# Products of the first layer in 26 multiplications: new order of the pairs, sums made when needed, additions that read PSUM

## Chip, cores and metric

The kernel runs on one core of one Trainium2 chip. The metric is device time in microseconds (us), the median of several executions. PE is the matrix engine (TensorE; PEld are its weight loads), DVE is VectorE, ACT is ScalarE, POOL is GpSimd, SP is SyncE, which here only issues DMAs.

## The reference

```python
# q, k, v: (8 batches, 12 heads, 448 rows, 64); all float32
q_n, k_n = rmsnorm(q, g_q), rmsnorm(k, g_k)      # over the 64
scores = q_n @ k_n.T / 8
attn = softmax(scores)
x = (attn @ v)           # -> (8 * 448 tokens, 12 * 64 = 768)
h = x @ w_in             # w_in: 768 x 2048
g = h * sigmoid(h)       # SiLU
out = g @ w_out          # w_out: 2048 x 768
```

## The kernel before, in words

Attention runs in 24 *couples* (a couple is two pairs of heads of one batch, four heads); six couples are two batches, a *group*. Function `visit(c)` emits the scores (line 852), their exponentials on ACT (857) and the weighted sums (889) of couple c; `between(c)` emits what lies between two couples: the flips of the next q and k (782, 786), the sums of the weights (903) and their totals (932), and two calls of `fill`. `fill` takes matmuls of the first layer (`x @ w_in`) from a generator, a quota of columns per call, and deals a list of other small steps evenly between them; what it emits, in this order, is the order of every engine's queue. So couples 6 to 11 carry the first layer of batches 0 and 1, couples 12 to 17 that of 2 and 3, couples 18 to 23 that of 4 and 5; batches 6 and 7 are done alone, when attention is over. Last comes `out = g @ w_out` (`quad`, `deep`), which the change doesn't touch.

The groups of couples 6 to 17 use seven products in place of eight (class `Seven`). From couple 18 on `products_in` (line 1359) runs a scheme of 26 products for a 4 x 2 by 2 x 4 block product. `room.chunk(i)`, i from 0 to 3, holds a quarter of w_in, and each chunk needs 26 left factors (quarters of the chunk and sums of them, 128 x 384), 26 right factors (quarters of x and sums of them, 128 x 672), and additions of the products:

- `LEFT_SUMS`, `form(i)` (line 1179): 18 sums per chunk on DVE (line 1217), after a `restore` on POOL (1201). They are spread by `dealt` over the fills of couples 13 to 20. Six slots in `room.sums` rotate; `keep` (1193) stores each factor on SP's queue into `lefts` in DRAM (1197), 26 stores of 192 KB per chunk, in the places that the order of pairs asks for. A slot that comes round again waits for its store to land.
- `Ring` (1262): loads the two left factors of a pair (384 KB, line 1288) from `lefts` on ACT's queue into the next free slot. It starts at the end of couple 17 with seven slots, and gets five more when attention is over.
- `RIGHT_SUMS`, `sum_right` (1251): 18 sums per group, `EARLY_SUMS` (four) on POOL at the end of couple 17 or 23, `LATE_SUMS` (eight on DVE, six on POOL, line 1255) around the start of the products.
- `products_in`: thirteen pairs per chunk. A pair has two products of three matmuls, which the trace shows as twelve of 224 columns, into one bank of PSUM. ACT copies the bank to SBUF (1390, 1395). `combine` (1313) makes, one pair later, the additions that `AFTER` lists, 38 per chunk; 18 of them are marked for POOL, the rest go to DVE (line 1339). In the group that runs alone (`direct`) some of them read PSUM. A finished pair of outputs goes through SiLU (1308) and is saved in `hidden` (1310).
- `bank` (1040): in couples 18 to 23 the products take two banks named mm in turn, at times one of the scores' buffers (sc); alone there are eight.

In the `LAGGED` couples (10, 12 to 16, 18 to 22) the division by the total of the weights comes one couple later: `sum_up` (907) makes the totals in a bank mm, two reciprocals of 128 x 224 (941) and a copy (947) follow on DVE, and four DMAs on SP's queue (950) swap rows between the two factors; `divide` (960) uses them in the next couple.

`rounder` and `early` bring W_out into the form the products need, in pieces of 128 x 384: a load on SP (188), two steps on ACT (`open`, 203 and 204), three on DVE (226 to 233) and one on POOL (237). `early`, the first eight pieces, runs by `rounds` in couples 21 to 23; the other 24 run beside the products alone, from `prepare_out` (1507).

Of the kernel before, what the change touches and what calls it, by code (L numbers as in the profile page):

```python
# [35 lines left out]
)  # L36
FACTORS_LEFT = (
    18, 23, 22, 20, 3, 24, 11, 10, 2, 4, 25, 1, 16, 8, 14, 13, 17, 5, 9, 15, 21, 12, 2, 19, 3, 6,
# [7 lines left out]
}  # L46
FACTORS_RIGHT = (
    11, 1, 4, 12, 4, 0, 16, 24, 0, 3, 6, 22, 21, 19, 13, 17, 15, 7, 9, 14, 8, 25, 18, 10, 23, 20,
)


AFTER = {
    4: ((16, 100, "-", 104, 0),),
    6: ((22, 103, "+", 106, 0), (1, 22, "-", 102, 1)),
    7: ((17, 107, "-", 22, 0),),
    8: ((17, 17, "+", 108, 0), (4, 104, "+", 108, 1), (0, 102, "+", 17, 1)),
    12: ((18, 112, "-", 104, 0),),
    13: ((3, 113, "-", 111, 1),),
    16: (
        (23, 116, "-", 113, 0), (18, 18, "-", 23, 0), (14, 23, "-", 105, 0),  # L60
        (12, 105, "+", 18, 1), (8, 17, "+", 18, 1),
    ),
    17: ((27, 114, "+", 117, 0), (20, 27, "-", 106, 0), (11, 109, "+", 117, 1), (9, 101, "+", 27, 1)),
    18: (
        (24, 118, "-", 115, 0), (19, 108, "+", 24, 0), (14, 14, "+", 24, 0),
        (13, 20, "-", 118, 1), (9, 9, "-", 118, 1),
    ),
# [7 lines left out]
}  # L75
# [567 lines left out]
def bounded(  # L643
# [20 lines left out]
    hidden = dram.tile([z.NF, P, z.B * S], F32, name="hidden")  # L664

# [5 lines left out]
    work = mem.tile([P, 16 * S + z.NK], F32, name="work")  # L671
    at = 0
# [10 lines left out]
    r = [piece(S) for _ in range(2)]  # L683
# [223 lines left out]
    def sum_up(c):  # L907
# [50 lines left out]
        yield [lambda: invert(0), lambda: (invert(1), spread())]  # L958
# [216 lines left out]
    PAIRS = len(FACTORS_LEFT) // 2  # L1175
    lefts = dram.tile([room.NC, PAIRS, P, 2 * K3], F32, name="lefts")
    formed = []

    def form(i, engines):
# [3 lines left out]
        s = room.sums((0, 1, 1, 3)[i])  # L1183
        tiles = w.rearrange("p (r k f m) -> p r k f m", r=HW, k=2, f=room.CHUNK)
        slots = [s[:, ds(n * K3, K3)] for n in range(6)]
        held, order = {}, []
# [6 lines left out]
        def keep(n):  # L1193
            for q, name in enumerate(FACTORS_LEFT):
                if name == n:
                    dst = lefts[i, q // 2, :, ds(q % 2 * K3, K3)]
                    nc.sync.dma_start(dst.rearrange("p (r m) -> p r m", r=HW), source(n))

        def restore():
            halves = w.rearrange("p (c m r k) -> p c m r k", c=z.NW, m=2, r=2)[:, 0:HW]  # L1200
            nc.gpsimd.tensor_tensor(
                out=halves[:, :, :, 1], in0=halves[:, :, :, 0], in1=halves[:, :, :, 1],
                op=ALU.subtract,
            )

        def one(k):
            name, x, op, y = LEFT_SUMS[k]
            a, b = source(x), source(y)
            later = {n for _, x, _, y in LEFT_SUMS[k:] for n in (x, y)} | set(order)
            busy = {n for n in later if n in held}  # L1210
            at = next(n for n, t in enumerate(slots) if not any(held[m] is t for m in busy))
            slot = slots.pop(at)
            slots.append(slot)
            for old in [o for o, t in held.items() if t is slot]:
                del held[old]
            held[name] = slot
            engines[k % len(engines)].tensor_tensor(  # L1217
                out=source(name), in0=a, in1=b, op=ALU.subtract if op == "-" else ALU.add
            )
            if k < 4:  # L1220
                for n in (2 * k, 2 * k + 1):
                    keep(n)
            if order:
                keep(order.pop())
            order.append(name)
            if k == len(LEFT_SUMS) - 1:
                keep(order.pop())
                formed.append(i)
# [22 lines left out]
    def sum_right(group, engine, *names):  # L1251

        def one(name):
            x, op, y = RIGHT_SUMS[name]
            engine.tensor_tensor(  # L1255
                out=right_of(group, name), in0=right_of(group, x), in1=right_of(group, y),
                op=ALU.subtract if op == "-" else ALU.add,
            )

        return [lambda name=name: one(name) for name in names]  # L1260

    class Ring:
# [15 lines left out]
        def more(self):  # L1278
            while self.n < (z.B // 2 - 2) * room.NC * PAIRS:
# [8 lines left out]
                nc.scalar.dma_start(slot, lefts[i, t])  # L1288
# [11 lines left out]
    pending, silent = [], []  # L1300
# [12 lines left out]
    def combine(now):  # L1313


        if not pending:
            return
        at, group, f0, names, last, places, fresh = pending.pop(0)
        for q in names:
            for k, (name, x, op, y, engine) in enumerate(AFTER.get(q, ())):  # L1320
                a, b = (
                    fresh[n] if n in fresh and (n not in at or n == 100 + q) else blocks[at[n]]
                    for n in (x, y)
                )
                engine = engine and x not in fresh and y not in fresh
                spent = [n for n in (x, y) if last[n] == (q, k)]
                if name < 16:
                    pair = name // 2
                    if pair not in places:
                        places[pair] = blocks.pair()  # L1330
                    at[name] = places[pair][name % 2]
                elif name not in at:
                    gone = [n for n in spent if n >= 16 and n in at]
                    if gone:
                        at[name] = at[gone[0]]
                        spent.remove(gone[0])
                    else:
                        at[name] = blocks.single()
                (nc.gpsimd if engine else nc.vector).tensor_tensor(  # L1339
                    out=blocks[at[name]], in0=a, in1=b, op=ALU.subtract if op == "-" else ALU.add  # L1340
                )
                for n in spent:
                    if n >= 16 and n != name and n in at:
                        blocks.release(at[n])
                if name < 16 and last[name] == (q, k) and last.get(name ^ 1, (99,)) <= (q, k):
                    pair = name // 2
                    silent.append((now + 1, f0 + pair // 2, group[pair % 2], places[pair]))

    def last_uses():
        last = {}  # L1350
        for q in range(len(FACTORS_LEFT)):
            for k, (name, x, _, y, _) in enumerate(AFTER.get(q, ())):
                for n in (name, x, y):
                    last[n] = (q, k)
        return last
# [3 lines left out]
    def products_in(group, beside=lambda: None, direct=False):  # L1359


        last = last_uses()
        kept = {
            n for q in AFTER for _, x, _, y, _ in AFTER[q] for n in (x, y)
            if n >= 100 and (not direct or q // 2 != (n - 100) // 2 or n < max(x, y) == 100 + q)
        }
        rows = list(carried)
        carried.clear()
        for i in range(room.NC):
            at, places = {}, {}  # L1370
            for t in range(PAIRS):
                slot = stream.next()
                o = bank(S)
                for h in range(2):
                    beside()
                    b = right_of(group, FACTORS_RIGHT[2 * t + h])
# [28 lines left out]
    def settle():  # L1405
        while pending:
            combine(clock[0])
        activate_some(10**9, len(silent))
# [927 lines left out]
```

## Time and profile before

| | us |
|---|---|
| median of 3 executions | 1360.36 (1358.47 to 1362.15) |
| the profiled execution | 1361.65, span 1359.9 |
| couples 0 to 11 (to 306.9 of the span) | 306.9 |
| couple 12, couple 13 | 33.3, 34.6 |
| couples 14 to 17 | 154.5 |
| couples 18 to 23 | 244.1 |
| products alone | 129.5 |
| W_out | 457.0 |

Over the whole span PE is busy 95%, DVE 78%, ACT 39%, POOL 34%, and the mean granted PE clock is 0.977. An engine's busy share is a mean over stages, so the table of stretches in the next part is read instead: PE's busy time against a stretch's length says how long it waited, and the granted clock whether it ran at less than full speed in between. A row of a timeline ends, in brackets, with the idle time of the engine before the instruction and what ended that. In a group of instructions stand the tile written and the tiles read, partitions x elements, the count, busy time and the mean of one, then idle time before them with its causes.

### The profile page before, as it was taken

How to read it: one execution, taken by the hardware profiler on the slowest of the kernel's cores; microseconds unless marked ns; L12 is line 12 of the kernel's file. 1: busy time of each engine (PE TensorE's matmuls, PEld its weight loads, DVE VectorE, ACT ScalarE, POOL GpSimd, SP SyncE). 2: the span in 40 equal slices, each digit the busy share in tenths (PEclk: the TensorE clock that was granted, in tenths of full speed). 3: DMA queues.
4: the chain of work that ended last, by engine and by line, in shares of the span. 5: the costliest groups of instructions: out<-in, count | busy, mean ns of one | idle time of the engine just before them, and what ended most of it. 6: DMA issues, size and time to landing. Idle time of an engine off the chain costs nothing.

```text
span 1359.9 us, 21894 instructions
## 1 busy us (share of the span) xinstructions
PE 1290.1 (95%) x7788; PEld 956.8 (70%) x7788; DVE 1059.4 (78%) x1848; ACT 532.1 (39%) x968; POOL 455.7 (34%) x325
## 2 busy tenths in 40 slices
PE   9999999999999887969798799899999999999998
PEld 5444444544444443857575699876999999999998
DVE  6989788767686776777586888779878787878785
ACT  7875666645454453644665335420000000000000
POOL 7755364433443245545363665420000000000000
PEclk9999999999999898979998899999999999999999
DMA  9664456535476566697765577971413232322311
GB/s 242 172 179 124 124 137 152 123 85 114 122 192 174 157 181 203 179 253 211 220 166 172 185 261 257 314 265 43 129 60 111 74 98 74 103 83 94 117 56 38
DMA packets 308923, 205.63 MB, mean 151 GB/s; under 512 B 207588, under 2 KB 283492, under 8 KB 308804
## 3 DMA queue, kind: packets, MB, share of 16 engines
q1 hardware_dynamic: 293200, 162.13, 42.5%
q10 hardware_dynamic: 15284, 41.10, 9.3%
q8 instruction: 64, 1.05, 0.3%
q0 software_dynamic: 320, 0.90, 0.2%
q14 instruction: 55, 0.45, 0.1%
HBM read 136.25 MB, written 61.73 MB: 146 GB/s over the span
## 4 chain that ended last, share of the span: by engine, by line
PE 40%; DVE 11%; DMA 5%; POOL 3%; issue 2%; ACT 2%; SPq 0%; ACTq 0%; DVEq 0%; POOLq 0%
PE alone L1651 22%; PE mm L1651 7%; PE av L889 3%; PE sc L852 2%; PE alone L1689 2%; DMA W<-lefts 2%; DVE W L1339 2%; DVE mixed L1339 1%; POOL W L1339 1%; PE alone L1378 1%; DVE work L903 1%; DVE W L1255 1%; PE mm L1689 1%; PE mm L1378 1%; DMA hidden<-W 1%
## 5 line engine op out<-in xcount | busy, mean ns | idle before, releaser
L857 ACT ACTIVATE work<-sc,rms 128x448 f32<-128x448 f32 x318 | 181.7, 634 | 89.1 <-PE sc L852 79.1
L852 PE MATMUL sc<-work 64*64 64x448 f32 x1344 | 172.7, 554 | 2.0 <-ACT work L857 1.2
L889 PE MATMUL av<-work,rows 64*64 64x448 f32 x1272 | 161.0, 560 | 8.6 <-DVE av L865 8.6
L630 POOL DMA_DIRECT2D out_dram<-mixed x2 | 1.2, 592 | 445.4 <-DVE mixed L1012 445.4
L903 DVE TENSOR_TENSOR work<-work 128x896 f32<-128x896 f32 (+1 forms) x110 | 122.9, 1149 | 34.8 <-PE av L889 34.3
L603 POOL TENSOR_TENSOR rms<-rms,minus_half 128x14 f32<-128x14 f32 (+4 forms) x40 | 99.2, 2482 | 100.2 <-DVE rms L599 96.2
L889 PEld LDWEIGHTS av<-work,rows 64*64 64x64 f32 x1272 | 67.6, 137 | 74.5 <-issue 26.1
L1651 PE MATMUL alone<-W,x 128*128 128x192 f32 x544 | 111.0, 326 | 0.0
L852 PEld LDWEIGHTS sc<-work 64*64 64x64 f32 x1344 | 60.8, 135 | 66.7 <-ACT work L857 26.8
L1065 PE MATMUL mm<-x,W 128*128 128x448 f32 x234 | 95.3, 543 | 1.8 <-DVE mixed L1012 1.8
L1651 PEld LDWEIGHTS alone<-W,x 128*128 128x128 f32 x544 | 92.2, 190 | 0.0
L1065 PE MATMUL mm<-sums_x,W 128*128 128x448 f32 x204 | 84.5, 548 | 5.8 <-DVE mixed L1012 5.8
L822 POOL TENSOR_TENSOR rms<-rms,minus_half 128x28 f32<-128x28 f32 x15 | 72.9, 4857 | 40.2 <-DVE rms L819 40.2
L1065 PEld LDWEIGHTS mm<-x,W 128*128 128x128 f32 x234 | 43.6, 190 | 46.9 <-issue 40.0
L1065 PEld LDWEIGHTS mm<-sums_x,W 128*128 128x128 f32 x204 | 38.1, 191 | 46.6 <-issue 35.9
L1661 ACT COPY sums_x<-alone 128x192 f32<-128x192 f32 x33 | 10.5, 317 | 141.6 <-PE alone L1651 136.7
L237 POOL TENSOR_TENSOR W<-W 128x512 int32<-128x512 int32 (+1 forms) x30 | 39.6, 1319 | 65.3 <-DVE W L233 41.1
L1065 PE MATMUL sc<-x,W 128*128 128x448 f32 x150 | 60.7, 540 | 0.0
L1665 ACT COPY x<-alone 128x192 f32<-128x192 f32 x34 | 10.8, 318 | 122.6 <-PE alone L1651 113.8
L1217 DVE TENSOR_TENSOR W<-W 128x384 f32<-128x384 f32 x72 | 44.8, 646 | 17.2 <-DMA lefts<-W 13.2
L575 DVE TENSOR_REDUCE rms<-rows 128x8 f32<-128x512 f32 (+2 forms) x50 | 32.0, 639 | 32.9 <-ACT rows L574 32.5
L1651 PE MATMUL alone<-W,work 128*128 128x192 f32 x244 | 56.3, 326 | 0.0
(381 smaller groups left out, 3026.7 us busy)
## 6 DMA issues: line engine op xcount, KB each, us to landing
W<-lefts ACTq DMA_DIRECT2D x68, 384.0 KB, 4.2
lefts<-W SPq DMA_DIRECT2D x104, 192.0 KB, 2.7
x<-hidden SPq DMA_DIRECT2D x14, 1024.0 KB, 5.3
hidden<-mixed SPq DMA_DIRECT2D x31, 448.0 KB, 3.2
W<-in_moe_w_in_dram SPq DMA_DIRECT2D x22, 512.0 KB, 6.1
rows<-in_moe_w_out_dram SPq DMA_DIRECT2D x24, 384.0 KB, 4.7
work<-lefts ACTq DMA_DIRECT2D x24, 384.0 KB, 5.1
hidden<-mixed SPq DMA_DIRECT2D x33, 224.0 KB, 4.3
```

The costliest lines, as they stand in the source:

```text
L237: nc.gpsimd.tensor_tensor(out=wi, in0=wi, in1=low, op=ALU.add)
L603: nc.gpsimd.tensor_tensor(out=t, in0=t, in1=half, op=ALU.pow)
L822: nc.gpsimd.tensor_tensor(out=f, in0=f, in1=minus_half.to_broadcast([P, n]), op=ALU.pow)
L852: nc.tensor.matmul(two[ds(half * D, D), h, 0:S], keys[rows, ts(half, D)], qT[rows, pair, :], start=True, stop=True,)
L857: nc.scalar.activation(left_weights(c)[:, h] if j == LEFT else weights(c, j)[:, i, h], two[:, h, 0:S], AF.Exp, scale=norm.column(c, i, h, j),)
L889: nc.tensor.matmul(sums[i][ds(h * D, D), :], v, w, start=(j == 0 and step == 1), stop=(j == LEFT - 1 and step == 1),)
L903: nc.vector.tensor_tensor(out=total, in0=total, in1=more, op=ALU.add)
L1065: nc.tensor.matmul(t, self.left(name, s), self.right(name, s), start=s == ends[0], stop=s == ends[1])
L1217: engines[k % len(engines)].tensor_tensor(out=source(name), in0=a, in1=b, op=ALU.subtract if op == "-" else ALU.add)
L1339: (nc.gpsimd if engine else nc.vector).tensor_tensor(out=blocks[at[name]], in0=a, in1=b, op=ALU.subtract if op == "-" else ALU.add)
L1651: nc.tensor.matmul(t, x[:, i], y, start=i == ORDER[0], stop=i == ORDER[-1])
L1689: nc.tensor.matmul(o, a[:, 2 * i + m, t], right_one(name, i)[:, m], start=n == 0, stop=n == len(steps) - 1,)
```

## The change

The scheme of 26 products stays. What it does:

- `STEPS` gives a new order of the pairs, `AFTER` a new order of the additions. An operand -1 or -2 is the second or first half of the pair's bank, -3 the whole bank; a name in brackets is a pair made by one instruction of 448 columns; "=" is a copy on ACT, five per chunk in all. The other 33 additions per chunk (28 of 224 columns, five of 448) all run on DVE, at once behind their pair's matmuls, and 17 of them read PSUM.
- `NEEDS`: the fourteen late sums of x are made on DVE by `products_in`, ahead of the first eleven pairs of chunk 0. The four early ones go to DVE too.
- `form`: sums are made three to an area, stored by one DMA of 576 KB; six quarters of the chunk are stored singly, so 12 stores per chunk. Chunks 0 and 3 have two areas, chunks 1 and 2 six. `restore` runs on DVE. A pair's load picks its two factors out of `lefts`, in two runs per partition. Chunk 3's forms lie in couples 18 to 21.
- The first seven loads of the ring go on SP's queue, three of them at the end of couple 16.
- In couples 18 to 22 the totals use a buffer sc; ACT copies them, one row of each goes by DMA into a tile of 128 x 14, DVE inverts that, and two DMAs spread it through DRAM (`totals`) to all partitions.
- The eight early pieces of W_out run in couples 22 and 23, their first load at the end of couple 21.

```diff
+STEPS = (
+    ((3, 22), (4, 4)),
+    ((5, 11), (7, 16)),
+    ((18, 2), (11, 0)),
...
+    ((25, 3), (6, 23)),
 )
+AFTER = (
+    ((16, "=", -2, 0), (17, "=", -1, 0),),
+    ((18, "=", -2, 0), (19, "=", -1, 0),),
+    ((20, "-", -2, 16), (21, "=", -1, 0), (4, "+", 16, -1),),
+    (((22, 23), "+", (18, 19), -3), (24, "-", 22, 19), (25, "-", 23, 17),),
...
+    (((34, 35), "-", (30, 31), -3), (36, "+", 26, 34), (37, "+", 35, 33), (8, "+", 29, 36), (2, "+", 30, 37),),
...
+    ((10, "+", -2, 37), (14, "-", 43, -1), (6, "-", -1, 46),),
 )
+NEEDS = ((9, 13), (10, 15), (21, 20), (19,), (8,), (14,), (17,), (25,), (22,), (18,), (23,))
...
-        elif c in LAGGED:
+        elif c in LAGGED and c < 3 * GROUP:
             t = ps_mm.tile([P, BANK], F32, name="mm")[:, 0:S]
...
-        yield [lambda: invert(0), lambda: (invert(1), spread())]
+        def gather():
+            nc.scalar.copy(r[0], t)
+            rows = r[0].rearrange("(n p) s -> n p s", n=4)[:, 0]
+            nc.sync.dma_start(spot, rows.rearrange("n (p e) -> n p e", p=P // 4))
+
+        def invert_all():
+            d = totals[c % 2]
+            nc.vector.reciprocal(out=spot, in_=spot)
+            nc.sync.dma_start(d.rearrange("n (p e) -> (n p) e", p=P // 4), spot)
+            source = d.rearrange("(h one i) s -> h one (i s)", one=1, i=2)
+            nc.sync.dma_start(both_r, source.to_broadcast([2, D, 2 * S]))
+
+        yield [gather, invert_all] if c in LAGGED else [lambda: invert(0), lambda: (invert(1), spread())]
...
+        free = (
+            (room.sums(0),), (room.sums(0), room.sums(1), room.chunk(0)),
+            (room.sums(0), room.sums(1), room.chunk(1)), (room.sums(3),),
+        )[i]
+        areas = [a[:, ds(k * 3 * K3, 3 * K3)] for a in free for k in range(2)]
...
         def one(k):
             name, x, op, y = LEFT_SUMS[k]
+            area = areas[k // 3 % len(areas)]
+            held[name] = area[:, ds(k % 3 * K3, K3)]
+            (plus if op == "+" else minus)(source(x), source(y), source(name))
+            if k < SIX:
+                kept = lefts[i, :, ds(k * K3, K3)].rearrange("p (r m) -> p r m", r=HW)
+                nc.sync.dma_start(kept, source(k + 1))
+            if k % 3 == 2:
+                nc.sync.dma_start(lefts[i, :, ds((SIX + k - 2) * K3, 3 * K3)], area)
...
-                nc.scalar.dma_start(slot, lefts[i, t])
+                a, b = sorted(position[n] for n in STEPS[t][0])
+                source = lefts[i].rearrange("p (n k) -> p n k", k=K3)[:, a : b + 1 : b - a]
+                queue.dma_start(slot.rearrange("p (n k) -> p n k", k=K3), source)
...
+        row = AFTER[t]
+        joined = tuple(a[0] for a in row if a[1] == "=")
+        if len(joined) == 2:
+            nc.scalar.copy(block(joined), both)
+        for k, (name, op, x, y) in enumerate(row):
...
+            a, b = operand(x), operand(y)
+            (plus if op == "+" else minus)(a, b, block(name))
...
+            for t, (_, rights) in enumerate(STEPS):
+                if i == 0 and t < len(NEEDS):
+                    run_all(sum_right(group, nc.vector, *NEEDS[t]))
+                o = bank(S)
...
                 now = clock[0] = clock[0] + 1
...
+                combine(t, at, places, o, group, i * room.CHUNK, now)
                 stream.done(slot)
-                combine(now)
...
-        21: (2, 7), 22: (2, 6), 23: (2, 6), 26: (3, 5), 27: (3, 5), 28: (3, 5), 29: (3, 4),
+        21: (2, 7), 22: (2, 6), 23: (2, 6),
     }
-    rounds = {30: 3, 31: 3, 32: 3, 33: 3, 34: 3, 35: 1}
+    dealt.update((i, (3, n)) for i, n in zip(range(25, 32), (4, 3, 3, 3, 3, 3, 0)))
+    rounds = {32: 4, 33: 4, 34: 4, 35: 4}
...
+        if c == OLD + GROUP - 2:
+            stream.add(room.sums(2))
+            stream.more(nc.sync)
         if c in LAGGED:
             lagging.extend(next(sum_up(c)))
+            if c >= 3 * GROUP:
+                lagging.pop(0)()
+                lagging.insert(0, lambda: None)
```

Keys of `dealt` and `rounds` are half couples: i is 2 (c - 6), plus 1 for the second fill of couple c.

More of the change, by code (lines that the diff above doesn't have):

```diff
@@ L664, in bounded @@
     hidden = dram.tile([z.NF, P, z.B * S], F32, name="hidden")
+    totals = [dram.tile([4, S], F32, name=f"totals{i}") for i in range(2)]
     sets = [mem.tile([P, 2 * z.NW * S], F32, name=f"x{i}") for i in range(2)]
@@ L671, in bounded @@
     work = mem.tile([P, 16 * S + z.NK], F32, name="work")
+    spot = mem.tile([P, 4 * S // P], F32, name="spot")
     at = 0
@@ L681, in bounded @@
     e = [piece(4 * S).rearrange("p (i h s) -> p i h s", i=2, h=2) for _ in range(3)]
-    r = [piece(S) for _ in range(2)]
+    both_r = piece(2 * S)
+    r = [both_r[:, ts(i, S)] for i in range(2)]
     extra, at = sets[1], 0
@@ L1174, in bounded, with form @@
     T = S // 2
-    PAIRS = len(FACTORS_LEFT) // 2
-    lefts = dram.tile([room.NC, PAIRS, P, 2 * K3], F32, name="lefts")
+    PAIRS = len(STEPS)
+    SIX = 6
+    position = {n: n - 1 for n in range(1, SIX + 1)}
+    position.update((t[0], SIX + k) for k, t in enumerate(LEFT_SUMS))
+    lefts = dram.tile([room.NC, P, len(position) * K3], F32, name="lefts")
     formed = []
-    def form(i, engines):
+    def form(i):
         w = room.chunk(i)
-        s = room.sums((0, 1, 1, 3)[i])
+        free = (
[3 more added lines that the diff above has]
+        areas = [a[:, ds(k * 3 * K3, 3 * K3)] for a in free for k in range(2)]
         tiles = w.rearrange("p (r k f m) -> p r k f m", r=HW, k=2, f=room.CHUNK)
-        slots = [s[:, ds(n * K3, K3)] for n in range(6)]
-        held, order = {}, []
+        held = {}
         def source(n):
@@ L1191, in source @@
             return held[n].rearrange("p (r m) -> p r m", r=HW)
[L1193 to L1197, printed above, removed]
         def restore():
             halves = w.rearrange("p (c m r k) -> p c m r k", c=z.NW, m=2, r=2)[:, 0:HW]
[L1201 to L1204, printed above, removed]
+            minus(halves[:, :, :, 0], halves[:, :, :, 1], halves[:, :, :, 1])
         def one(k):
             name, x, op, y = LEFT_SUMS[k]
[L1208 to L1225, printed above, removed]
+            area = areas[k // 3 % len(areas)]
[6 more added lines that the diff above has]
+                nc.sync.dma_start(lefts[i, :, ds((SIX + k - 2) * K3, 3 * K3)], area)
             if k == len(LEFT_SUMS) - 1:
-                keep(order.pop())
                 formed.append(i)
@@ L1276, in add, with more @@
             return new
-        def more(self):
+        def more(self, queue=nc.scalar):
             while self.n < (z.B // 2 - 2) * room.NC * PAIRS:
@@ L1311, in activate_some @@
             blocks.release(*two)
[L1313 to L1355, printed above, removed]
-    clock = [0]
[L1359 to L1366, printed above, removed]
+    def named(*operands):
+        return {n for x in operands for n in (x if isinstance(x, tuple) else (x,)) if n >= 0}
@@ new lines, in bounded, with combine, block, operand @@
+    last_use = {}
+    for t, row in enumerate(AFTER):
+        for k, (_, op, x, y) in enumerate(row):
+            if op != "=":
+                last_use.update(dict.fromkeys(named(x, y), (t, k)))
+    def combine(t, at, places, o, group, f0, now):
+        both = o.rearrange("p (two s) -> p two s", two=2)
+        def block(name):
+            if isinstance(name, tuple):
+                at.update(zip(name, blocks.pair()))
+                return blocks.two(*(at[n] for n in name))
+            if name < 16:
+                pair = name // 2
+                if pair not in places:
+                    places[pair] = blocks.pair()
+                at[name] = places[pair][name % 2]
+            else:
+                at[name] = blocks.single()
+            return blocks[at[name]]
+        def operand(n):
+            if isinstance(n, tuple):
+                return blocks.two(*(at[m] for m in n))
+            return both if n == -3 else o[:, ts(n + 2, T)] if n < 0 else blocks[at[n]]
+        row = AFTER[t]
[3 more added lines that the diff above has]
+        for k, (name, op, x, y) in enumerate(row):
+            if op == "=":
+                if len(joined) == 1:
+                    nc.scalar.copy(block(name), operand(x))
+                continue
+            a, b = operand(x), operand(y)
+            (plus if op == "+" else minus)(a, b, block(name))
+            for n in named(x, y):
+                if n >= 16 and last_use[n] == (t, k):
+                    blocks.release(at.pop(n))
+            if not isinstance(name, tuple) and name < 16 and name ^ 1 in at:
+                pair = name // 2
+                silent.append((now + 1, f0 + pair // 2, group[pair % 2], places[pair]))
@@ L1367, in products_in @@
+    clock = [0]
+    def products_in(group, beside=lambda: None):
         rows = list(carried)
@@ L1405, in settle @@
     def settle():
-        while pending:
-            combine(clock[0])
         activate_some(10**9, len(silent))
@@ L2117, in bounded @@
     slots = prepare_out()
-    run(products_in(group, lambda: run_all(next(slots, ())), direct=True))
+    run(products_in(group, lambda: run_all(next(slots, ()))))
     for more in slots:
```

81 lines of the change are left out of this document (23 added, 58 removed), and 31 rows, old and new, of tables (AFTER, LEFT_SUMS, RIGHT_SUMS).

## Prediction

> **What bounds the kernel now.** I read busy time by stretches, cut at the first score product of each couple of head pairs (couples 14 to 23) and at the end of attention. Columns: window, length, busy time (instructions) of PE, PEld, DVE, ACT, POOL, granted clock, DMA share, GB/s.
>
> ```profile
> 374.80:408.00 33.20, 33.20 (x186) 16.64 (x182) 27.47 (x41) 17.13 (x28) 14.10 (x7) 1.00 0.70 189
> 408.00:449.00 41.00, 35.16 (x188) 16.39 (x185) 26.35 (x40) 18.94 (x29) 13.54 (x6) 0.94 0.66 176
> 449.00:487.50 38.50, 34.60 (x184) 16.99 (x182) 27.24 (x39) 16.60 (x26) 15.10 (x7) 0.97 0.59 174
> 487.50:529.30 41.80, 33.89 (x188) 16.76 (x185) 35.96 (x44) 15.78 (x26) 20.16 (x11) 0.96 0.61 168
> 529.30:564.20 34.90, 33.88 (x224) 24.23 (x224) 22.93 (x30) 20.05 (x33) 14.77 (x7) 0.95 0.81 233
> 564.20:610.70 46.50, 35.77 (x234) 27.35 (x230) 31.45 (x46) 22.77 (x41) 29.37 (x25) 0.86 0.77 205
> 610.70:648.20 37.50, 34.14 (x236) 26.78 (x232) 28.65 (x44) 16.35 (x29) 18.75 (x14) 0.94 0.79 222
> 648.20:689.90 41.70, 35.42 (x232) 27.41 (x234) 25.77 (x41) 26.05 (x47) 19.23 (x17) 0.92 0.77 218
> 689.90:727.80 37.90, 32.88 (x229) 25.48 (x229) 29.89 (x43) 23.19 (x42) 22.47 (x21) 0.95 0.67 183
> 727.80:773.40 45.60, 37.03 (x253) 25.97 (x249) 33.96 (x42) 18.14 (x33) 21.98 (x22) 0.87 0.44 137
> 773.40:902.90 129.50, 122.28 (x625) 119.93 (x626) 109.55 (x208) 54.64 (x118) 70.99 (x71) 0.98 0.80 273
> ```
>
> Couple 14 is the measure: PE is never idle in 33.2 us, and VectorE is idle 33.2 - 27.5 = 5.7 us of them. Couples 15 to 17 do the same work in 121.3, that is 21.7 over 3 x 33.2. Couples 18 to 22 need 32.9 of PE each (the least row) and couple 23 needs 37.0: 201.4 against 244.1, so 42.7 over. The products alone (773 to 903) are nearly full. What follows, 457 us of W_out, the change leaves alone. So 64 us lie in nine couples, and the long waits there name their reason (start, duration, instruction, idle time before it and what ended it):
>
> ```profile
> 445.50 1.11 PE L1065 MATMUL mm<-sums_x,W 128*128 128x448 f32 x1 [5.84 <-DVE mixed L1012]
> 528.77 0.42 PE L818 MATMUL sc<-rms,ident 64*64 64x28 f32 x4 [7.80 <-DVE rms L805]
> 609.04 0.98 PE L932 MATMUL mm<-work,ones 128*32 128x448 f32 x4 [6.91 <-ACT mixed L1390]
> 680.32 0.74 PE L1378 MATMUL mm<-sums_x,W 128*128 128x224 f32 x1 [5.48 <-ACT W L1390]
> 771.62 1.02 PE L889 MATMUL av<-work,rows 64*64 64x448 f32 x4 [8.57 <-DVE av L865]
> 604.89 1.15 DVE L1217 TENSOR_TENSOR W<-W 128x384 f32<-128x384 f32 x2 [5.58 <-DMA lefts<-W]
> 608.55 0.56 DVE L1217 TENSOR_TENSOR W<-W 128x384 f32<-128x384 f32 x1 [1.49 <-DMA lefts<-W]
> 678.35 0.54 ACT L203 ACTIVATE W<-W 128x384 int32<-128x384 uint32 x1 [7.96 <-DMA W<-in_moe_w_out_dram]
> L1217 DVE TENSOR_TENSOR W<-W 128x384 f32<-128x384 f32 x72 | 44.8, 646 | 17.2 <-DMA lefts<-W 13.2 <-POOL W L1201 3.4
> ```
>
> PE waits for VectorE, or for a ScalarE that waits for VectorE. VectorE in turn stands in its forming of weight sums (L1217), 13.2 us until a store of an earlier sum frees the slot and 3.4 for GpSimd's restore. The reader is to see the pairs: 604.89 on VectorE leads to 609.04 on PE.
>
> **The change part by part. Prices first:**
>
> ```profile
> 774.61 0.85 DVE L1255 TENSOR_TENSOR W<-x 128x672 f32<-128x672 f32 x1
> 774.84 2.09 POOL L1255 TENSOR_TENSOR sums_x<-x 128x672 f32<-128x672 f32 x1 [2.21 <-DVE x L963]
> 775.49 2.16 DVE L1255 TENSOR_TENSOR W<-x,W 128x672 f32<-128x672 f32 x1
> L1339 DVE TENSOR_TENSOR W<-W,alone 128x224 f32<-128x224 f32 x18 | 6.6, 380 | 2.3 <-POOL W L1339 2.1
> L1339 DVE TENSOR_TENSOR mixed<-W 128x224 f32<-128x224 f32 x3 | 1.1, 379 | 0.0
> L1012 DVE TENSOR_TENSOR mixed<-mm,mixed 128x448 f32<-128x448 f32 x57 | 34.7, 609 | 11.2 <-PE mm L1065 4.9 <-ACT mixed L1455 3.5 <-POOL mixed L1089 1.9
> 487.50:529.30 41.80, 10.22 (x12) 0.96 0.61 168
> 529.30:564.20 34.90, 3.00 (x5) 0.36 (x1) 0.95 0.81 233
> 529.30:773.40 244.10, 46.27 (x79) 56.71 (x70) 0.91 0.70 198
> 773.40:902.90 129.50, 41.53 (x110) 33.26 (x41) 0.98 0.80 273
> 529.30:773.40 244.10, 7.94 (x8) 16.86 (x10) 0.91 0.70 198
> 773.40:902.90 129.50, 11.89 (x8) 12.43 (x6) 0.98 0.80 273
> L941 DVE RECIPROCAL work<-mm 128x224 f32<-128x224 f32 x10 | 15.5, 1548 | 1.8 <-PE mm L932 1.8
> L947 DVE COPY work<-work 128x448 f32<-128x448 f32 x6 | 3.9, 651 | 0.2
> L1378 PEld LDWEIGHTS alone<-x,W 128*128 128x128 f32 x72 | 13.6, 190 | 0.0
> 527.17 6.25 ACTq L1288 DMA_DIRECT2D W<-lefts  x7
> hidden<-mixed SPq DMA_DIRECT2D x31, 448.0 KB, 3.2
> lefts<-W SPq DMA_DIRECT2D x104, 192.0 KB, 2.7
> W<-lefts ACTq DMA_DIRECT2D x68, 384.0 KB, 4.2
> ```
>
> The window rows are busy times of single lines: L1217 in couple 17; L1339 in couple 18, in 18 to 23 and alone (DVE, then POOL); L1255 in the last two of these.
>
> The first three rows show a collision: a VectorE addition of 672 columns takes 0.85 us by itself and 2.16 while GpSimd adds. A 224-column addition takes 0.38, from SBUF alone or with one operand in PSUM. Every addition that leaves GpSimd therefore costs VectorE 0.38 and frees its neighbours.
>
> *Forms in threes (couples 13 to 21).* Stores fall from 26 to 12 per chunk, and slots from six in rotation to eighteen for chunks 1 and 2. There no sum waits for a store. Where there are two areas (chunks 0 and 3), one comes round half a couple later, against 2.7 us of landing for a third of what it holds. Couple 15's 5.84 goes down to about 1, and with it most of the cold clock (0.94 of 41.0): -6.5. In couple 16 the restore moves to VectorE, which no longer waits for GpSimd: -3. In couple 17 twelve sums fall from 10.2 to 12 x 0.56 = 6.7, but four sums of x come over from GpSimd (4 x 0.86 = 3.4), so its 7.8 us wait mostly stays: -1.5. Together -11. The bounds are -5 (one wait alone) and -21.7 (all of it).
>
> *Additions from PSUM.* A chunk has thirteen pairs, each freeing its bank before by ScalarE's copy. Now a chunk has 28 narrow additions and 5 of 448 columns on VectorE, 28 x 0.38 + 5 x 0.61 = 13.7 us, and 5 copies on ScalarE instead of about 13. Four chunks are 54.8; VectorE had 46.3 in couples 18 to 23 and 41.5 alone, with GpSimd's 56.7 and 33.3 beside it.
>
> [...]
>
> *Lazy sums of x.* All fourteen go to VectorE, in the first eleven pairs of chunk 0, two pairs or more ahead of their use: 14 x 0.86 = 12.0 against 7.9 and 11.9 before. GpSimd loses 16.9 and 12.4.
>
> *Lagged totals (couples 18 to 22).* Ten reciprocals (15.5) and five copies (5 x 0.65 = 3.3) go, five reciprocals of 14 columns (1 together) and a ScalarE copy come. SP now waits twice, for the small reciprocal and for the landing of the totals. Queued behind are v loads, saves of hidden and stores of forms, all wanted a quarter of a couple later or more. I take nothing; without that cover it is the last rival.
>
> *Loads.* The first seven leave ScalarE's queue (6.25 us of issue at couple 18's start) for SP's. Each later load is two runs: between 0 and 2 x 2.7 - 4.2 = 1.2 us more to land, behind seven slots. I take 0; in the stretch alone, with five slots more, up to 6.
>
> *W_out pieces.* They leave couple 21. The second one's load is still issued only after the first is rounded, so of 680.32's 5.48 I keep 4 in couple 22.
>
> Sum for couples 18 to 23. VectorE had 172.7; + 54.8 - 46.3; - 15.5 - 3.3 + 1; sums + 12.0 + 3.4 (early ones in couple 23) - 7.9; comes to 170.9. With 5.7 idle per couple that is 205.1, level with PE's 201.4, so no slack for uneven loads. Couple 18 is uneven: 22.9 - 3.0 - 7.9 + 7.0 (8.7 pairs) + 12 sums x 0.86 + four form steps (2.6) = 31.9, with idle time 37.6 against 34.9 now. It gets slower; 19 to 21 gain. I add 4 (W_out), 4 (half of 771.62's, as GpSimd's part is gone) and 8 of the remaining 22 us of small waits and cold clock: 221, or -23. The bounds are 201 and 256 (second rival).
>
> Sum alone. PE needs 624 x 0.19 = 118.6. VectorE comes to 109.6 - 41.5 + 54.8 - 11.9 + 12.0 = 123.0, less what GpSimd's absence saves. The first chunk holds 13.7 + 12.0 + 14.0 (a quarter of the other 56.2) = 39.7 against 29.7 of PE; two pairs of lead are 4.6, relief 2, so +3. The bounds are -8 and +12.
>
> Total: -11 - 23 + 3 = -31. From the profiled execution, 1361.65 (span 1359.9 and 1.75 around it; 1.3 above the median of 1360.36), that is **1330**.
>
> **Rivals.**
>
> *All waits gone.* PE becomes the only bound, as the lower bounds of the three stretches have it: 1361.7 - 21.7 - 42.7 - 8 = 1289. For it: couple 14 shows that it can be. Against it: VectorE at 205.1.
>
> *VectorE in the turn of the banks.* Couples 18 to 23 have two banks for products. A bank now comes free after VectorE's additions, which stand in order behind flips, sums and rounding; ScalarE's copy stood behind little. If VectorE lags by more than one pair (12 x 0.19 = 2.3 us), every pair shows its additions: 52 x 13.7 / 13 = 54.8 on 201.4, or 256, which is +12. Alone the sums show as well: +12. With -11 from the forms it is 1375, slower. For it: 528.77 and 771.62, where PE waits for a late VectorE. Against it: mean load.
>
> *Nothing much.* Only the forms' waits go, and couple 18, couple 23 and the first chunk alone give back 8 of the 11: 1358. That would also be the outcome if the waits for stores were merely handed to the next late instruction.
>
> [...]
>
> **How the numbers follow.** Forecast 0.68, all waits gone 0.08, banks 0.12, nothing 0.08, few engines 0.04. A difference under 0.3% (4 us) is what a measurement of this kernel can't tell from none. Forecast, first and last rival are faster, with a quarter of "nothing" (0.82); the rest of it is the same (0.06); banks are slower (0.12). The range runs from 1304 (two thirds of the way from the forecast to those lower bounds) to 1358 (the third rival); outside lie 1289 and 1375, 0.20.
>
> **What would show it.** Right: no wait of VectorE for lefts<-W; couple 15 near 34, couple 18 longer than 34.9, couple 19 under 38; GpSimd without adds; VectorE near 170 and 115 in the two stretches. [...]

## The result, and the profile after

The changed kernel takes 1369.78 us (median of 4, 1368.62 to 1370.43) against 1360.56 for the kernel before on the same chip: ratio 1.0068, 95% interval 1.0050 to 1.0085. It is slower by 0.7%; the forecast was 1330. The profiled execution took 1370.43, span 1368.4.

First the same stretches as before, cut at the same events (couples 14 to 23, then the products alone), in the kernel after; columns as in the prediction:

```profile
372.90:412.10 39.20, 33.97 (x192) 16.86 (x188) 24.22 (x39) 17.67 (x29) 13.86 (x7) 0.99 0.62 175
412.10:452.20 40.10, 35.16 (x176) 16.00 (x176) 23.93 (x39) 18.46 (x29) 11.67 (x5) 0.96 0.59 167
452.20:489.90 37.70, 33.65 (x188) 16.51 (x184) 24.95 (x38) 17.74 (x29) 12.98 (x6) 1.00 0.60 176
489.90:534.30 44.40, 35.97 (x192) 17.46 (x189) 31.15 (x46) 17.77 (x29) 13.53 (x7) 0.96 0.61 174
534.30:573.70 39.40, 34.49 (x229) 25.68 (x229) 28.97 (x48) 17.09 (x29) 9.72 (x4) 0.96 0.86 231
573.70:614.00 40.30, 32.65 (x228) 25.01 (x228) 26.56 (x51) 20.24 (x35) 9.02 (x4) 0.99 0.71 199
614.00:657.00 43.00, 36.98 (x232) 27.30 (x233) 26.26 (x53) 17.35 (x31) 9.38 (x4) 0.89 0.71 193
657.00:698.40 41.40, 36.04 (x231) 27.37 (x231) 19.97 (x36) 17.86 (x31) 9.27 (x4) 0.88 0.68 197
698.40:741.00 42.60, 34.67 (x224) 25.71 (x224) 24.81 (x49) 20.42 (x39) 10.38 (x6) 0.94 0.62 190
741.00:783.60 42.60, 35.80 (x253) 25.61 (x250) 32.03 (x62) 19.07 (x34) 4.23 (x4) 0.98 0.53 162
783.60:911.40 127.80, 122.99 (x625) 120.28 (x626) 109.01 (x233) 48.95 (x100) 26.14 (x24) 0.97 0.84 279
```

Couple 14, without a wait before (33.2), now takes 39.2; couples 15 to 17 take 122.2 together (121.3 before), couples 18 to 23 249.3 (244.1). Yet VectorE has become lighter in all but couple 18 of them (19.97 of 41.40 in couple 21, 25.77 before), and no engine is full. The reader should then look at the engine that does no work of its own, SP. Its timeline about couple 15 in the kernel after (start, duration of the issue, instruction), followed by what the other engines waited for:

```profile
420.50 0.56 SPq L976 DMA_DIRECT2D work<-totals  x1
...
425.58 7.06 SPq L419 DMA_DIRECT2D rows<-in_v_dram  x4
432.74 4.06 SPq L360 DMA_DIRECT2D rows<-in_q_dram  x8
436.90 0.90 SPq L1124 DMA_DIRECT2D hidden<-mixed  x2
...
439.61 0.53 ACT L1105 COPY mixed<-mm 128x448 f32<-128x448 f32 x1 [8.87 <-DMA hidden<-mixed]
...
440.19 2.52 PE L1085 MATMUL mm<-sums_x,W 128*128 128x448 f32 x6 [1.85 <-ACT mixed L1105]
```

The kernel before, same place, same view:

```profile
420.67 2.95 SPq L414 DMA_DIRECT2D rows<-in_v_dram  x4
423.72 4.05 SPq L355 DMA_DIRECT2D rows<-in_q_dram  x8
427.88 0.90 SPq L1104 DMA_DIRECT2D hidden<-mixed  x2
```

The four v loads take 7.06 us to issue in place of 2.95, so all that SP queues behind them slips: the save of `hidden` goes out at 436.90, 9 us after 427.88 (the couple itself began 4 us later). ScalarE waits 8.87 us for the buffer that this save frees, and PE for ScalarE. What blocks the issue stands in the waits of SP's queue over couples 14 to 23 (us in total, times, longest). Its two longest rows:

```profile
SPq L974 <- DVE spot L973: 27.7, 9, 4.8
SPq L419 <- DMA work<-totals: 23.2, 8, 3.1
```

The first, the wait for the small reciprocal, is there in the faster version below as well (30.1); the second is not. It is the wait for line 976, which spreads the inverted totals over 128 partitions: one DMA of 448 KB whose leading axis is 2. In the trace its 128 packets of 3584 bytes take 0.14 us each (median) and start between 421.84 and 431.58: 128 x 0.14 / 9.7 = 1.8 DMA engines at work on average, out of 16. The share of the DMA engines in tenths, over 40 slices of 420.5 to 432 us, shows it as a long row of ones, broken where other transfers get through:

```profile
DMA  0000012223536411131142146111111646411111
```

It runs in eleven couples. Here the description of the change above and the prediction are wrong: the new totals serve all `LAGGED` couples (10, 12 to 16, 18 to 22), not 18 to 22 alone; only the place of `gather` and its buffer sc are special from couple 18 on.

### The profile page after: what moved, and what is told of

Its sections match the earlier page's. It is cut to its first block, busy times and chain, and to the rows that moved or that the text cites. A ratio compares the mean times of both kernels' runs of the same rounds, so it can differ in the third digit from the quotient of the medians.

```text
span 1368.4 us, 21624 instructions
## 1 busy us (share of the span) xinstructions
PE 1293.0 (94%) x7788; PEld 955.7 (70%) x7788; DVE 1027.0 (75%) x1922; ACT 515.9 (38%) x931; POOL 321.1 (23%) x189
## 4 chain that ended last, share of the span: by engine, by line
PE 77%; DVE 10%; DMA 7%; ACT 2%; SPq 2%; issue 2%; ACTq 0%; POOL 0%; DVEq 0%; POOLq 0%
PE alone L1651 22%; PE av L897 9%; PE sc L860 9%; PE mm L1085 9%; PE mm L1651 7%; PE alone L1392 5%; PE sc L1085 4%; PE mm L1392 4%; PE alone L1689 2%; DVE W L1029 2%; DMA work<-totals 2%; PE mm L940 2%; PE sc L1392 1%; DVE mixed L1032 1%; DVE work L911 1%
## 5 line engine op out<-in xcount | busy, mean ns | idle before, releaser
L911 DVE TENSOR_TENSOR work<-work 128x896 f32<-128x896 f32 (+1 forms) x110 | 119.3, 1116 | 39.1 <-PE av L897 38.6
L1029 DVE TENSOR_TENSOR W<-W 128x384 f32<-128x384 f32 (+3 forms) x123 | 67.4, 573 | 7.7 <-DMA lefts<-W 6.3
L1085 PEld LDWEIGHTS mm<-sums_x,W 128*128 128x128 f32 x204 | 37.7, 190 | 49.8 <-issue 35.5
L1032 DVE TENSOR_TENSOR rows<-rows,x 128x192 f32<-128x192 f32 x72 | 25.7, 358 | 37.4 <-ACT x L1665 35.6
```

Of the source, the lines that this page charges most:

```text
L911: nc.vector.tensor_tensor(out=total, in0=total, in1=more, op=ALU.add)
L1029: nc.vector.tensor_tensor(out=out, in0=a, in1=b, op=ALU.subtract)
L1032: nc.vector.tensor_tensor(out=out, in0=a, in1=b, op=ALU.add)
L1085: nc.tensor.matmul(t, self.left(name, s), self.right(name, s), start=s == ends[0], stop=s == ends[1])
```

## The experiments

Theory A: the one-DMA spread costs the time. Its rival B: the spread is harmless, and the time goes with VectorE's new work and the banks that it frees late. All times stand beside 1357.98 to 1359.21 for the kernel before, run with them.

**The spread in two DMAs.** Only this differs from the kernel after:

```diff
-source = d.rearrange("(h one i) s -> h one (i s)", one=1, i=2)
-nc.sync.dma_start(both_r, source.to_broadcast([2, D, 2 * S]))
+source = d.rearrange("(h i) s -> h (i s)", i=2)
+for h in range(2):
+    nc.sync.dma_start(both_r[ds(h * D, D)], source[h : h + 1].to_broadcast([D, 2 * S]))
```

> The changed kernel, its spreading of the lagged totals cut into two DMAs of 64 partitions each, so that the leading axis of both sides is 64 and no longer 2. Theory A (the spreading rides few DMA engines and clogs SP's queue in all eleven lagged couples): packets of 3584 B run over about 1.5 us instead of 9.8, the v and q loads behind them are issued some 5 us earlier, and the time falls by 15 to 30 us to 1340 to 1355. Theory B (VectorE's additions hold the two banks): 1365 to 1370, nothing gained in couples 18 to 23.

Measured: 1327.42, ratio 0.9759 (0.9732 to 0.9785), below even A's figure. The spread's packets now lie within 2.4 us, on nearly all engines (DMA share in tenths, 415 to 419 us):

```profile
DMA  0000000000000097449899899499799589999657
```

Its stretches, couples 14 to 23 and alone:

```profile
374.50:408.30 33.80, 33.57 (x192) 16.94 (x189) 24.98 (x39) 17.04 (x27) 13.48 (x6) 1.00 0.68 184
408.30:442.50 34.20, 33.45 (x178) 15.85 (x178) 24.77 (x39) 18.51 (x29) 11.88 (x5) 1.00 0.73 198
442.50:476.80 34.30, 33.48 (x184) 16.43 (x180) 24.94 (x38) 18.35 (x30) 12.57 (x6) 1.00 0.67 198
476.80:519.50 42.70, 35.98 (x190) 17.06 (x187) 30.20 (x46) 17.26 (x27) 13.89 (x7) 0.96 0.72 201
519.50:559.90 40.40, 35.55 (x228) 25.42 (x229) 29.07 (x48) 17.16 (x29) 9.70 (x4) 0.92 0.74 202
559.90:598.00 38.10, 34.27 (x228) 25.54 (x229) 26.56 (x51) 19.03 (x33) 9.08 (x4) 0.95 0.73 207
598.00:635.10 37.10, 33.97 (x228) 25.43 (x229) 26.17 (x53) 18.75 (x32) 9.29 (x4) 0.96 0.84 221
635.10:670.50 35.40, 33.78 (x232) 25.96 (x233) 19.58 (x36) 18.31 (x32) 9.37 (x4) 0.95 0.82 229
670.50:704.90 34.40, 32.54 (x228) 24.91 (x228) 24.42 (x48) 20.51 (x38) 10.38 (x6) 0.98 0.75 228
704.90:748.40 43.50, 36.71 (x251) 25.60 (x249) 32.16 (x63) 19.06 (x34) 4.23 (x4) 0.93 0.56 173
748.40:872.80 124.40, 121.10 (x629) 119.10 (x626) 109.00 (x233) 49.39 (x100) 26.25 (x24) 0.99 0.85 284
```

VectorE's busy time per couple is within 1 us of that of the kernel after (24.94 and 24.95 in couple 16, 26.56 and 26.56 in couple 19), and the couples are shorter by 2 to 8 us in all but couples 18 and 23. Work was not the difference; waits were. The profiled execution took 1332.33, 5 us above the median; where stages are compared below, the other profiles stand beside it.

**The old totals in the kernel after** (condition `c in LAGGED` for the bank and the old list of reciprocals put back, the early call in couples 18 to 22 dropped).

> The changed kernel with the totals as before: two reciprocals of 128 x 224, a copy and four DMAs, in a bank mm. Theory A: faster than the changed kernel by 10 to 25 us, and slower than the two-DMA version by what the reciprocals cost (up to 10). Theory B: VectorE gets 18 us more work, so slower than the changed kernel, about 1375 to 1385.

Measured: 1328.22, 0.9782 (0.9750 to 0.9814), the same as with two DMAs. So the new totals as such are worth nothing that can be measured, although they take reciprocals and copies off VectorE: in couples 18 to 23 it is busy 175.3 us here and 158.0 with two DMAs, and these couples are no longer for it (222.6 and 228.9). Couple 17 takes 39.8 here and 42.7 there.

**The new totals alone in the kernel before**, with one DMA and with two:

```diff
+    totals = [dram.tile([4, S], F32, name=f"totals{i}") for i in range(2)]
+    spot = mem.tile([P, 4 * S // P], F32, name="spot")
...
-        yield [lambda: invert(0), lambda: (invert(1), spread())]
+        yield [gather, invert_all] if c in LAGGED else [lambda: invert(0), lambda: (invert(1), spread())]
```

> The kernel before with nothing but the new totals (one DMA spreads them). Theory A: the clogged queue alone makes it slower than before by 10 to 30 us, 1370 to 1390. Theory B: VectorE is relieved of reciprocals and the banks still come free by ScalarE's copy: faster than before, 1340 to 1355.

> The kernel before with the new totals and the spreading in two DMAs. Both theories: faster than before, 1340 to 1355; under theory A well below the version with one DMA (20 us or more), under theory B the same as that one within 4 us.

Measured: 1396.29 with one DMA, 1.0278 (1.0251 to 1.0305); 1361.51 with two, 1.0025 (1.0004 to 1.0046). Both theories had expected a gain with two, 1340 to 1355; there is none. The one DMA costs 1396.3 - 1361.5 = 35 us in a kernel without any of the other edits. It shows where that kernel is sensitive, in VectorE's sums of weights (last columns: idle time before them and what ended it), one DMA first:

```profile
L1232 DVE TENSOR_TENSOR W<-W 128x384 f32<-128x384 f32 x66 | 41.4, 649 | 33.9 <-DMA lefts<-W 31.5 <-POOL W L1216 1.7
```

With two:

```profile
L1233 DVE TENSOR_TENSOR W<-W 128x384 f32<-128x384 f32 x66 | 41.5, 655 | 14.1 <-DMA lefts<-W 11.9 <-POOL W L1217 1.7
```

Stores of 192 KB are waited for 31.5 us in place of 11.9, while VectorE's own work is equal.

**One DMA, issued by GpSimd.** Is it only SP's queue, whose later issues stand behind the spread (A1), or do the two engines hold up transfers of any queue (A2)?

```diff
-            nc.sync.dma_start(both_r, source.to_broadcast([2, D, 2 * S]))
+            nc.gpsimd.dma_start(both_r, source.to_broadcast([2, D, 2 * S]))
```

> The changed kernel with its one DMA that spreads the totals issued by GpSimd, and no longer by SP. The leading axis stays 2. Theory A1 (the slow DMA fills SP's way to its engines, and the v, q, hidden and form transfers behind it are issued late): SP is free again, 1325 to 1340. Theory A2 (the totals come late, or two engines of the sixteen hold up every transfer whichever queue it comes from): stays at 1360 to 1370.

Measured: 1366.64, 1.0049 (1.0032 to 1.0067): all but 3 us of the loss stays, so A1 falls as the only cause. The spread, now on another queue, lands 12.7 us after its issue (DMA view, median):

```profile
work<-totals POOLq DMA_DIRECT2D x11, 448.0 KB, 12.7
```

With two DMAs, on SP's queue, it took 4.0:

```profile
work<-totals SPq DMA_DIRECT2D x22, 224.0 KB, 4.0
```

In the run with GpSimd's queue SP's eight loads of q, which come after the spread in time alone, are stuck in issue for 10.51 us, against 4.05 in the kernel before. SP's timeline of that run:

```profile
421.84 10.51 SPq L360 DMA_DIRECT2D rows<-in_q_dram  x8
```

The loads of v, also on SP's queue, are issued without delay in this run but land late. This run over 418 to 432 us, then the kernel before over 415 to 432 us (DMA view, last number the median from issue to landing):

```profile
rows<-in_v_dram SPq DMA_DIRECT2D x4, 64.0 KB, 10.4
rows<-in_v_dram SPq DMA_DIRECT2D x6, 64.0 KB, 2.1
```

And ScalarE's waits for saves of `hidden` in couples 14 to 23 are those of the kernel after, not of the version with two DMAs. This run, the kernel after, two DMAs:

```profile
ACT mixed L1105 <- DMA hidden<-mixed: 14.1, 4, 8.9
ACT mixed L1105 <- DMA hidden<-mixed: 14.9, 4, 8.9
ACT mixed L1106 <- DMA hidden<-mixed: 3.3, 1, 3.3
```

That the later transfers' packets stand behind the spread's in its few engines (1.8 at work in the kernel after) would explain it, but is argued, not shown; that transfers of another queue are held up is shown. One thing is new in this run: GpSimd's own queue now stands before the spread until `totals` is stored, 19.9 us in three waits, so part of the time may come from there.

The remaining runs change other parts, all with the spread in two DMAs (1327.42).

**Forms of the kernel before** (sums in the old order and stored singly, restore on GpSimd, a pair's load in one run per partition again).

```diff
-            if k % 3 == 2:
-                nc.sync.dma_start(lefts[i, :, ds((SIX + k - 2) * K3, 3 * K3)], area)
+            if order:
+                keep(order.pop())
+            order.append(name)
```

> The version with the totals spread in two DMAs, with the forms of the weights as in the kernel before: six rotating slots, 26 stores per chunk, the restore on GpSimd. Theory of the prediction (threes are worth 11 us in couples 15 to 17 and the waits of couples 19 and 20 for lefts<-W): 1338 to 1350, couple 15 near 40 again. Rival (the forms were not the cause, the queue's order is): within 4 us of 1327.

Measured: 1343.40, 0.9886 (0.9865 to 0.9907), so the new forms, with the loads that belong to them, are worth 16 us. Couples 15, 16 and 17 take 38.6, 37.7 and 44.7 here against 34.2, 34.3 and 42.7: 4.4, 3.4 and 2.0.

**Two areas for all four chunks.**

```diff
-        areas = [a[:, ds(k * 3 * K3, 3 * K3)] for a in free for k in range(2)]
+        areas = [a[:, ds(k * 3 * K3, 3 * K3)] for a in free[:1] for k in range(2)]
```

> The version with the totals spread in two DMAs, with two areas for the forms of all chunks instead of six for chunks 1 and 2. Theory of the prediction (with two areas, stored by one DMA, a slot comes round late enough): within 3 us of 1327. Rival (the eighteen slots are what removed the waits for stores): couples 15 to 17 lose 5 us or more, 1333 to 1340, and VectorE waits for lefts<-W again.

Measured: 1332.23, 0.9807 (0.9783 to 0.9831). Couples 15 to 17, where the forms of chunks 1 and 2 lie, take 111.4 against 111.2, and VectorE waits for a store only once in couples 14 to 23, 0.8 us: the eighteen slots are not what helps there. The whole kernel is slower by more than the 3 us expected, but the intervals of the two touch; the rest is unclear.

**Sums of x up front, as before**, ten of the eighteen on GpSimd again. In this kernel some products of chunk 0 use a right factor before its sum is made.

```diff
-                if i == 0 and t < len(NEEDS):
-                    run_all(sum_right(group, nc.vector, *NEEDS[t]))
...
+    for engine, names in zip((nc.vector, nc.gpsimd), LATE_SUMS):
+        run_all(sum_right(group, engine, *names))
```

> The version with the totals spread in two DMAs, with the sums of x as in the kernel before: four on GpSimd in couples 17 and 23, fourteen on VectorE and GpSimd at the start of the products. Theory of the prediction (lazy sums make couple 18 longer, front sums collide with GpSimd): couple 18 falls from 40 to about 36, the products alone rise by 3, couple 17 falls by 2: 1320 to 1328. Rival (the front sums hold up the first products): 1330 to 1340.

Measured: 1334.88, 0.9824 (0.9804 to 0.9845), so sums made when needed, all on VectorE, gain some 7 us. The prediction's theory had expected the opposite, 1320 to 1328. Couple 18 takes 45.8 with the sums up front; with the lazy sums it takes 40.4, and between 36.9 and 42.6 in the profiles of the other versions without the one DMA.

**ScalarE copies each bank first** in couples 18 to 23, so that no addition holds it.

```diff
+        if group[0] < z.B - 2 and any(a[1] != "=" for a in row):
+            spare_two = blocks.pair()
+            nc.scalar.copy(blocks.two(*spare_two), both)
```

> The version with the totals spread in two DMAs, with every bank whose products are added copied by ScalarE first in couples 18 to 23, and the additions reading the copy. Rival of the prediction (banks held by VectorE's additions are on PE's path): 1315 to 1324. Prediction (they are not, and ScalarE gets 32 copies of 0.5 us more): 1327 to 1337.

Measured: 1327.22, 0.9772 (0.9749 to 0.9796): no difference. The turn of the two banks sets no time here.

**Eight additions per chunk, SBUF only, back on GpSimd** in couples 18 to 23.

```diff
-            (plus if op == "+" else minus)(a, b, block(name))
+            if pooled and not isinstance(name, tuple) and x not in (-1, -2) and y not in (-1, -2) and name < 16:
+                nc.gpsimd.tensor_tensor(
...
```

> The version with the totals spread in two DMAs, with eight of the sixteen additions per chunk that read SBUF alone (the outputs 0, 8, 2, 12, 3, 5, 1, 7) given to GpSimd in couples 18 to 23. Theory of the prediction (an addition on GpSimd costs VectorE more by collision than it saves): 1328 to 1337. Rival (VectorE is the bound there, and 32 x 0.38 = 12 us less of it counts): 1317 to 1325.

Measured: 1328.97, 0.9781 (0.9759 to 0.9804): no difference. But the load hardly moved either: VectorE is busy 155.5 in these couples in place of 158.0, although 32 additions of 0.38 (12 us) went, while its other steps got slower (last section). GpSimd's busy time rises from 52.0 to 79.1.

**The totals gathered at the couple's end from couple 12 on** (`c >= 2 * GROUP`), meant to take away VectorE's waits for `spot`.

> The version with the totals spread in two DMAs, with ScalarE's copy and the first small DMA put at the end of the couple for couples 12 to 16 too, as they stand for 18 to 22. If VectorE's wait for the gathered totals (2 to 7 us in front of the small reciprocal) is on PE's path: 1320 to 1325, couple 17 near 40 instead of 42.7. If it is covered by the weighted sums that VectorE would wait for anyway: within 2 us of 1327.

Measured: 1330.90, 0.9788 (0.9772 to 0.9805); couple 17 takes 42.3 against 42.7. The waits did not go away: the version with two DMAs has the first row, this run the second, so what the wait costs stays open.

```profile
DVE spot L973 <- DMA spot<-work: 18.0, 5, 7.8
DVE spot L973 <- DMA spot<-work: 16.7, 6, 7.5
```

**Old totals up to couple 16, new ones from 18 on.**

```diff
-        yield [gather, invert_all] if c in LAGGED else [lambda: invert(0), lambda: (invert(1), spread())]
+        yield [gather, invert_all] if c in LAGGED and c >= 3 * GROUP else [lambda: invert(0), lambda: (invert(1), spread())]
```

> The version with the totals spread in two DMAs, with the new totals from couple 18 on alone and the old ones in couples 10 and 12 to 16. If VectorE's saved reciprocals count only where it is the bound: couple 17 near 39.8 as in the version with all old totals, 1322 to 1327, the fastest so far. Else within 2 us of 1327.

Measured: 1325.87, 0.9763 (0.9743 to 0.9783): the fastest figure, but not apart from 1327.42. Couple 17, where the longest wait for `spot` lies, takes 39.7, as with all old totals; with the new ones there it takes 42.3 to 44.7 in every profile of the changed kernel and its versions. Both beat both kernels, the kernel before by 2.4% (0.9759; 0.9732 to 0.9785).

Not tried: the one DMA with other leading axes (4, 8, 64). The version with two DMAs changes the axis and the number of DMAs at once. That few engines carried the one DMA is in its packets' times; that its axis of 2 is the reason is argued from these and from the pairs of kernels with one DMA and two.

## Why the prediction was wrong

**The step that failed** is "Lagged totals": "I take nothing; without that cover it is the last rival." That cover was not there. What matters is not SP's two waits in its own queue, which the step weighed, but the transfer itself, which held up the loads and saves behind it (the v loads' issue 7.06 us for 2.95, the save of `hidden` out 9 us later). It measured 1369.8 - 1327.4 = 42 us in the kernel after and 35 in the kernel before, 3.9 and 3.2 for each of eleven uses.

**Few engines, the last rival in the chances (0.04), was the cause.** No row of the profile before told the number of engines; the kernel after has 1.8 at work for 9.7 us, and with two DMAs the packets lie within 2.4 us on nearly all. The shape, a leading axis of 2, was in the diff, and nothing in the profile spoke against it. The count was wrong as well: the step has the new totals in couples 18 to 22, five uses for eleven, a plain misreading of one condition in the diff. The 42 us do not fall evenly: from couple 14 to 23 single ones differ by -1 to 8 us between one DMA and two. And it acted through late transfers, not through a late division: no wait of VectorE for the spread totals stands in the trace. It made saves of `hidden`, loads of q and stores of sums late: in couples 14 to 23 ScalarE waits 14.9 us for the saves, and 14.1 for loads of q.

**Forms in threes: right.** Forecast -11 in couples 15 to 17 (-6.5, -3, -1.5). Taking them out gave back 4.4, 3.4 and 2.0 there, 9.8 together. The other 6 of the whole kernel's 16 us can't be placed: the later stages scatter by as much from version to version. Its reason was partly wrong: two areas do as well as six in these couples. In the kernel with two DMAs VectorE waits for no store of a sum; in the kernel after it waits 6.3 us for them:

```profile
L1029 DVE TENSOR_TENSOR W<-W 128x384 f32<-128x384 f32 x46 | 25.4, 577 | 6.5 <-DMA lefts<-W 6.3
```

So the sign given for being right, no such wait, failed for the same cause as the rest.

**Couples 18 to 23: the size was near, the reason wrong.** With two DMAs they take 228.9 in that run's profile, and 220.4 to 224.6 in those of the six other versions that come within 5 us of it (forecast 221). The forecast came from VectorE at 170.9; it was 158.0, the sum of the DVE column. The additions themselves were priced well: the two lines of plus and minus are busy 63.5 in these couples with two DMAs, less 9.6 for steps of forms and 1.0 for W_out 52.9, against 54.8. Those of 224 columns that read PSUM take 377 to 389 ns, those from SBUF alone mostly 384 to 391. But VectorE's load does not set the time: with the old totals it is 175.3, and the couples take 222.6. What fills the 19 to 27 us above PE's 201.4 is still open; the granted clock is 0.95 over these couples with two DMAs (0.92 to 0.98 in a single one). Couple 18 got slower, as said (forecast 37.6, before 34.9), with 40.4, and 36.9 to 42.6 in the six; but not for its reason, the lazy sums, since sums up front make it 45.8. Couple 19 is at 38.1.

**Alone: +3 forecast.** It takes 124.4 in the run with two DMAs, where the kernel before took 129.5. Over all ten profiles with the new order of products and sums the mean is 127.4 (123.6 to 130.1), over three with the old 128.7 (127.8 to 129.5). So no loss shows, and a gain of 1 us can't be told from the scatter. VectorE's 109.0 (forecast 123.0) leaves slack.

**The rival of the banks fell** with the copy first in couples 18 to 23 and, alone, with the stretches, as did "nothing much" and "all waits gone". Take the failed step out, and the forecast of 1330 stands beside 1327.4. Part of that is luck: in that run's profile the three stages gain 10, 15 and 5, where the forecast had 11, 23 and -3, so that two misses of 8 cancel. In the six others couples 18 to 23 gain 19 to 24, nearer to the 23.

## What to carry to other kernels

For each DMA that a change adds, write down its leading axis before any time: here a broadcast that begins with an axis of 2 kept 1.8 engines at work for 9.7 us, and in two DMAs that each begin with 64 partitions it took 2.4 (the axis and the number of DMAs changed together). Price such a transfer by all that is in flight beside it, whichever queue issues it, not by its own user. And multiply by the number of places that the condition in the code gives, read from the code.

## What the runs showed of the hardware that was not expected

- A 448 KB DMA that landed 12.7 us after its issue held up transfers of another queue: SP's issue of eight small loads grew from 4.05 to 10.51 us and loads of v landed in 10.4 us in place of 2.1 while GpSimd's DMA ran, and moving it to that queue saved only 3 us of 42.
- Work on VectorE that falls away can be worth nothing here: ten reciprocals of 1.55 us (couples 18 to 22) became five of 0.24, VectorE's busy time in couples 18 to 23 fell from 175.3 to 158.0, and the time of the kernel didn't move (1328.2 with the old totals, 1327.4 with the new).
- VectorE's W_out steps got faster with GpSimd's additions gone: these rows of the kernel before and after, eight steps each, show 503 and 355 ns for the same shape. With eight additions per chunk back on GpSimd, and nothing else changed, it is 526 (third row) against 352.

```profile
L226 DVE TENSOR_SCALAR W<-W 128x384 f32<-128x384 f32 x8 | 4.0, 503 | 3.7 <-ACT W L204 3.7
```

```profile
L231 DVE TENSOR_SCALAR W<-W 128x384 f32<-128x384 f32 x8 | 2.8, 355 | 8.4 <-ACT W L209 8.4
```

```profile
L231 DVE TENSOR_SCALAR W<-W 128x384 f32<-128x384 f32 x8 | 4.2, 526 | 0.1
```
